# Attention and two feed-forward layers on one core: v tiles in borrowed weight slots, a rewritten order of the first group, split conversions

## The chip, the cores and the metric

The kernel runs on one core of one Trainium2 chip. The metric is the device time of one execution in microseconds (us), of which several were taken; less is better. One execution was also recorded by the hardware profiler, and all rows below come from that one.

## The reference, cut to what matters

```python
# q, k, v: (batch 4, heads 8, seq 576, head_dim 64); all float32
scores = q @ k.T / 8                  # heads 0-3: window of 32; heads 4-7: 32 keys at distance 0, 4, 8 ... 124
attn = softmax(where(mask, scores, -1e9)) @ v
x = attn.transpose(0, 2, 1, 3).reshape(2304, 512)
h = x @ w_in                          # 512 -> 2048
x = (h - tanh(h)) @ w_out             # 2048 -> 512
out = (((x @ w1) * (x @ w2)) @ w3) @ w_out2    # 512 -> 1024, 1024 -> 1024, 1024 -> 512
```

## The kernel before, in words

**Split numbers.** Each matrix operand of the feed-forward layers is held as a high part and a low part in TensorE's own 32-bit format, and a product is three matmuls (high by high, high by low, low by high). A weight arrives as raw 64-bit words and must be converted on the core: ScalarE takes an absolute value (word `a` of the list below, `cv_abs`), VectorE does two pairs of bit operations (`b` and `c`, lines 148 to 161, `cv_bits`), ScalarE writes the high part (`i`, line 166), GpSimd the low part (`o`, line 169). A weight lands in one of two staging buffers, so the third weight can be loaded only when the `c` of the first is done.

**Attention** works on 12 units (a batch and a third of the sequence), each of two types: `p`, the plain window, and `d`, the dilated one. For a unit and type, SyncE loads q and k (`q`), then v (`v`); TensorE makes the masked scores (`s`, lines 466 and 478), VectorE takes the maximum and subtracts it (`M`), ScalarE takes the exponential (`E`), VectorE sums and inverts (`N`), GpSimd multiplies (`m`), TensorE transposes (`T`, line 522), ScalarE copies (`C`), TensorE multiplies by v (`P`, line 553), ScalarE and VectorE write the high and low part of the result into `X` (`X`, `L`). The scores of the first three units are made type by type, of later units both types together.

**First layer pair.** The 16 chunks of w_in and w_out go in four groups of 3, 4, 4 and 5 chunks. In the first group the tokens go in seven tiles of 256 and one of 512, in later groups in tiles of 512 and 256. One step `i` is one chunk on one token tile: `h` (12 matmuls, line 596), `t` (tanh), `g` (subtract, line 644), `G` and `k` (high and low part), `y` (12 matmuls, line 686); after the last chunk of a group `Y` and `Z` add the four y banks into `Y` (lines 704 to 708).

**Who sets the order.** Up to the end of the first group every engine's instructions follow one list written out by hand, `ORDER`: each word is one of the letters above with a unit or step number, `S` is a run of dummy matmuls on a zero tile (`spin`, line 715), `K` prepares the masks and `w` loads a weight. Each engine runs its own instructions in that order, SyncE its loads as well: a load that must wait for a buffer holds back all loads behind it. Later a loop goes through the steps: for step i it issues `h`, `t`, `g`, `G`, then `tick()` (which converts the next weight), then the low part, then `y` of step i-1 and its four adds. The second layers follow as a loop over products, which the change does not touch.

**Buffers.** q, k and v of the first units lie in the not yet used `Y`, as far as there is room; later ones in three rotating buffers each. Before the change three of the first unit's v tiles found room there; the other three took the three rotating v buffers. `WG` holds 16 weight slots of 2 KB a partition, from the start on.

Of the kernel before, what the change touches and what calls it, by code (L numbers as in the profile page):

```python
# [45 lines left out]


ORDER = """
q0p S10 q1p K0 K1 q1d s0p S2 M0p q2p s1p E0p N0p S6 v1p M1p m0p T0p E1p q0d S1 C0p N1p s2p m1p v0p
M2p T1p S4 C1p q2d E2p s0d N2p s1d m2p v0d M0d P0p E0d M1d w0 P1p X0p N0d E1d T2p w1 X1p N1d m0d s2d  # L50
C2p L1p m1d L0p T0d v2p M2d a0 S5 C0d v1d b0 E2d T1d c0 a1 q3p S2 P2p N2d i0 P0d o0 b1 X2p w2 C1d S6
X0d q3d L2p m2d L0d P1d c1 T2d X1d v2d a2 L1d i1 b2 h0 C2d w3 o1 c2 s3 t0 q4p g0 i2 P2d M3 G0 o2 q4d
a3 h1 X2d k0 b3 E3 y0 w4 t1 c3 v3p g1 i3 s4 L2d G1 o3 N3 v3d a4 k1 h2 M4 w5 m3p m3d T3p t2 v4p g2
C3p b4 h3 G2 q5p c4 E4 P3p t3 a5 g3 k2 T3d N4 X3p v4d h4 i4 C3d o4 L3p q5d b5 t4 P3d y1 g4 m4d X3d
c5 v5p h5 G3 q6p L3d m4p i5 s5 k3 o5 t5 w6 g5 T4p M5 y2 q6d C4p P4p Y2 Z2 E5 q7p T4d y3 C4d N5 X4p
v5d P4d G4 m5p L4p G5 a6 m5d T5p v6p X4d b6 s6 C5p k5 c6 w7 T5d P5p M6 k4 q7d C5d y4 X5p i6 L5p E6
w8 o6 L4d h6 a7 N6 q8p y5 t6 b7 g6 m6d s7 c7 G6 Y5 v6d a8 Z5 k6 i7 w9 h7 b8 M7 m6p y6 q8d t7 o7 g7
E7 T6p c8 h8 q9p G7 a9 N7 k7 C6p P5d t8 w10 b9 s8 X5d m7d L5d g8 v7p m7p c9 G8 y7 q9d k8 T6d a10 P6p
C6d M8 q10p h9 X6p L6p E8 y8 b10 v7d t9 g9 P6d N8 G9 w11 Y8 k9 s9 X6d Z8 m8d L6d v8p m8p c10 T7p
q10d h10 C7p P7p t10 q11p g10 T7d G10 X7p h11 k10 M9 C7d v8d T8p t11 P7d g11 E9 w12 L7p s10 X7d N9  # L60
C8p v9p L7d m9p P8p m9d q11d T8d X8p y9 C8d L8p M10 v9d h12 G11 k11 E10 P8d t12 N10 s11 X8d v10p L8d
m10p g12 m10d h13 y10 t13 g13 y11 G12 k12 T9p Y11 Z11 h14 C9p G13 T9d k13 t14 y12 g14 C9d M11 y13
G14 k14 E11 P9p N11 P9d X9p v10d L9p m11p T10p X9d h15 v11p C10p L9d m11d T10d t15 P10p g15 C10d y14
X10p v11d G15 L10p k15 P10d Y14 Z14 T11p X10d h16 C11p L10d y15 t16 g16 G16 P11p k16 h17 X11p L11p
y16 t17 g17 G17 h18 k17 y17 t18 g18 G18 T11d k18 Y17 Z17 h19 C11d P11d t19 g19 y18 X11d G19 L11d Q0
k19 i8 h20 i9 o8 i10 y19 t20 o10 a11 g20 G20 b11 h21 k20 c11 y20 o9 t21 w13 i11 g21 o11 G21 h22 Z20
a12 Y20 k21 b12 a13 y21 t22 b13 g22 c12 G22 h23 k22 c13 i12 y22 t23 o12 i13 g23 G23 o13 h24 k23 y23
t24 g24 G24 k24 Y23 Z23
"""


# [1062 lines left out]
```

## Time and profile before

| what | value |
|---|---|
| median of 3 runs | 815.25 us (814.08 to 817.67) |
| profiled execution | 815.71 us, span of its instructions 813.9 us |
| TensorE matmuls busy | 788.7 us, 97% of the span |
| VectorE busy | 559.5 us, 69% |
| ScalarE busy | 292.4 us, 36% |
| GpSimd busy | 159.9 us, 20% |
| moved by DMA | 115.58 MB |

TensorE is the busiest engine, but its busy time includes 36 dummy matmuls and is an average over stages. The rows further down give it by stage: the start, the rest of the attention, the loop over the later groups, and the second layers.

### The profile page before, as it was taken

The numbers are of one execution on the slowest core, as the hardware profiler recorded it, in microseconds if no ns is written. First come the engines' busy times: TensorE is split into PE (matmuls) and PEld (weight loads), VectorE is DVE, ScalarE is ACT, GpSimd is POOL, SyncE is SP. The second block draws the span as 40 slices with busy tenths as digits, with TensorE's granted clock in tenths as the row PEclk, the third lists the DMA queues.
The fourth block names the chain that finished last, engine by engine and source line by source line (L and its number), as shares of the span: only waits on it lengthen the run. The fifth ranks groups of instructions, "written<-read, shape, count | busy, mean of one in ns | idle before, by whom it ended". The sixth has DMA issues, their size and how long they took to land.

```text
span 813.9 us, 14227 instructions
## 1 busy us (share of the span) xinstructions
PE 788.7 (97%) x5623; PEld 689.5 (85%) x5628; DVE 559.5 (69%) x911; ACT 292.4 (36%) x543; POOL 159.9 (20%) x155
## 2 busy tenths in 40 slices
PE   7798999999999999999999999999999999999998
PEld 4577889888878888788878788889998999899996
DVE  4889833758888888987888989964454444644441
ACT  3555645443444444443434433421123111311111
POOL 3344322600022000221022222311111111201011
PEclk9999999999999999999999999999999999999999
DMA  8999942213455254642354325187402761146402
GB/s 258 289 266 288 287 107 60 76 55 104 124 162 170 76 150 125 190 138 84 103 170 142 102 82 178 58 291 256 146 1 65 226 202 38 39 154 201 139 1 77
DMA packets 62018, 115.58 MB, mean 142 GB/s; under 512 B 6400, under 2 KB 27008, under 8 KB 61952
## 3 DMA queue, kind: packets, MB, share of 16 engines
q1 hardware_dynamic: 61664, 114.32, 46.3%
q8 instruction: 44, 0.72, 0.4%
q10 hardware_dynamic: 288, 0.36, 0.2%
q14 instruction: 22, 0.18, 0.1%
HBM read 95.26 MB, written 19.40 MB: 141 GB/s over the span
## 4 chain that ended last, share of the span: by engine, by line
PE 79%; DVE 11%; DMA 5%; issue 2%; SPq 1%; ACT 1%; ACTq 0%; DVEq 0%
PE h L596 22%; PE pr L935 22%; PE y L686 20%; PE o L998 6%; PE pr L998 6%; DVE a L158 2%; PE x L553 2%; DVE a L161 2%; DMA q<-in_qz 2%; DMA Y<-in_qz 2%; DVE a L152 1%; DVE a L148 1%; DVE th L644 1%; DVE Y L704 1%; DVE gs L658 1%
## 5 line engine op out<-in xcount | busy, mean ns | idle before, releaser
L596 PE MATMUL h<-X,WG 128*128 128x512 f32 (+1 forms) x662 | 129.0, 342 | 3.1 <-DVE th L644 3.0
L686 PE MATMUL y<-gs,LT 128*128 128x512 f32 (+1 forms) x520 | 123.0, 369 | 3.2 <-DVE Y L704 2.5
L596 PEld LDWEIGHTS h<-X,WG 128*128 128x128 f32 x662 | 105.4, 191 | 18.2 <-DVE th L644 3.7
L686 PEld LDWEIGHTS y<-gs,LT 128*128 128x128 f32 x520 | 92.0, 188 | 21.5 <-issue 4.5
L686 PE MATMUL y<-gs,WG 128*128 128x256 f32 (+1 forms) x548 | 108.4, 332 | 1.2 <-DVE Y L704 0.9
L596 PE MATMUL h<-X,LT 128*128 128x512 f32 (+1 forms) x471 | 104.7, 369 | 0.0
L596 PEld LDWEIGHTS h<-X,LT 128*128 128x128 f32 x471 | 82.8, 189 | 15.0
L686 PEld LDWEIGHTS y<-gs,WG 128*128 128x128 f32 x548 | 85.1, 189 | 12.2 <-issue 1.4
L644 DVE TENSOR_TENSOR th<-h,th 128x512 f32<-128x512 f32 (+1 forms) x83 | 51.2, 617 | 58.8 <-ACT th L638 58.6
L638 ACT ACTIVATE th<-h 128x512 f32<-128x512 f32 (+1 forms) x83 | 44.8, 540 | 124.5 <-PE h L596 123.3
L161 DVE SCALAR_TENSOR_TENSOR a<-st,a 128x512 uint32<-128x512 uint32 x68 | 80.8, 1188 | 2.3
L935 PE MATMUL pr<-X 128*128 128x384 f32 x435 | 81.9, 335 | 0.0
L935 PE MATMUL pr<-X,LT 128*128 128x384 f32 x405 | 80.3, 335 | 0.0
L935 PEld LDWEIGHTS pr<-X 128*128 128x128 f32 x435 | 76.3, 188 | 0.5
L651 ACT ACTIVATE gs<-th 128x512 fp32r<-128x512 f32 (+1 forms) x83 | 47.7, 576 | 70.2 <-DVE th L644 67.1
L935 PEld LDWEIGHTS pr<-X,LT 128*128 128x128 f32 x405 | 71.4, 188 | 1.3
L972 DVE TENSOR_TENSOR u<-pr,u 128x384 f32<-128x384 f32 x72 | 40.1, 557 | 45.6 <-PE pr L935 38.9
L990 POOL TENSOR_TENSOR Y<-w,v 128x384 f32<-128x384 f32 x24 | 24.4, 1019 | 213.1 <-DVE w L972 213.1
L948 ACT ACTIVATE cs<-u 128x384 fp32r<-128x384 f32 x24 | 12.6, 526 | 148.6 <-DVE u L972 148.6
L143 ACT ACTIVATE a<-st 128x512 f32<-128x512 f32 x68 | 45.5, 669 | 31.1 <-DMA st<-in_w_out 10.0
L169 POOL TENSOR_TENSOR LT<-a,LT 128x512 fp32r<-128x512 f32 x18 | 25.2, 1402 | 157.1 <-ACT LT L166 155.1
L158 DVE SCALAR_TENSOR_TENSOR a<-st,a 128x512 uint32<-128x512 uint32 x68 | 53.6, 789 | 2.1
(132 smaller groups left out, 1077.4 us busy)
## 6 DMA issues: line engine op xcount, KB each, us to landing
st<-in_w SPq DMA_DIRECT2D x28, 512.0 KB, 3.5
LT<-p SPq DMA_DIRECT2D x56, 256.0 KB, 4.4
X<-p SPq DMA_DIRECT2D x56, 256.0 KB, 4.9
st<-in_w_in SPq DMA_DIRECT2D x16, 512.0 KB, 4.4
st<-in_w_out SPq DMA_DIRECT2D x16, 512.0 KB, 4.2
p<-WG SPq DMA_DIRECT2D x30, 256.0 KB, 4.6
q<-in_qz SPq DMA_DIRECT2D x19, 384.0 KB, 6.6
p<-LT SPq DMA_DIRECT2D x26, 256.0 KB, 4.6
```

Of the source, the lines that this page charges most:

```text
L143: nc.scalar.activation(out=a.bitcast(F32), in_=st[:, :, 1].bitcast(F32), func=ACTF.Abs)
L158: nc.vector.scalar_tensor_tensor(out=a, in0=st[:, :, 1], scalar=0xC0000000, in1=a, op0=ALU.bitwise_and, op1=ALU.bitwise_or)
L161: nc.vector.scalar_tensor_tensor(out=a, in0=st[:, :, 0], scalar=29, in1=a, op0=ALU.logical_shift_right, op1=ALU.bitwise_or)
L169: nc.gpsimd.tensor_tensor(out=lo, in0=a.bitcast(F32), in1=hi.bitcast(F32), op=ALU.subtract)
L596: nc.tensor.matmul(out=ps, lhsT=a[sel[0]], rhs=b[sel[1]], start=(start and i == 0), stop=(i == n - 1), **kw)
L638: nc.scalar.activation(out=th[:, :tn], in_=gst[i][:, :tn], func=ACTF.Tanh)
L644: nc.vector.tensor_tensor(out=th[:, :tn], in0=ps[:, :tn], in1=th[:, :tn], op=ALU.subtract)
L651: nc.scalar.activation(out=gs[:, 0, :tn], in_=th[:, :tn], func=ACTF.Copy)
L686: nc.tensor.matmul(out=y[k], lhsT=wt[sel[0]][:, 128 * k:128 * k + 128], rhs=gs[:, sel[1], tn * m:tn * m + tn], start=(cs[m] == 0 and n == ...
L935: nc.tensor.matmul(out=ps[:, :TP], lhsT=s[e][:, 128 * k:128 * k + 128], rhs=(hi, lo)[f][1][k], start=start and n == 0, stop=n == 5, skip_g ...
L972: nc.vector.tensor_tensor(out=out, in0=ps[:, :TP], in1=x, op=op)
L998: nc.tensor.matmul(out=tiles[m], lhsT=cs[e][:, 128 * m:128 * m + 128], rhs=WW[j][f], start=begin and n == 0, stop=end and n == 2,)
```

## The change

Four edits. (1) `WG` is cut to six slots; in the bytes of the other ten a pool of six v tiles holds v of the first batch (units 0 to 2, both types), and the ten slots are opened in the same bytes by `more_slots()` when the fourth weight needs them. (2) `ORDER` is written anew, without any `S`. (3) Of the four mask casts of line 363, two go to ScalarE, with the cast of the identity. (4) In the loop `tick()` is cut in two: the first pair of bit operations stays where it was, the second pair comes after the four adds of the step before.

```diff
+NF = 6
...
-WG = big.tile([128, NW, 512], F32R, name="WG")
+WG = big.tile([128, NF, 512], F32R, name="WG")
...
-free = deque(WG[:, i, :] for i in range(NW))
+free = deque(WG[:, i, :] for i in range(NF))
...
-X0d q3d L2p m2d L0d P1d c1 T2d X1d v2d a2 L1d i1 b2 h0 C2d w3 o1 c2 s3 t0 q4p g0 i2 P2d M3 G0 o2 q4d
+P0d o0 X2p L2p o1 X0d i2 M3 P1d L0d X1d E3 a3 L1d q4p q4d h0 v2d s4 N3 C2d P2d w4 b3 t0 g0 h1 G0 c3
...
-    def tick():
+    halfway = []
+
+    def tick_begin():
         busy = bitsed and split()
         if not busy and absed and len(free) >= slots_for(absed[0][0]) + reserve[0]:
             key, st, a = absed.popleft()
-            cv_bits(st, a)
+            cv_bits(st, a, 0)
+            halfway.append((key, st, a, [free.popleft() for _ in range(slots_for(key))]))
+
+    def tick_end():
+        if halfway:
+            key, st, a, slots = halfway.pop()
+            cv_bits(st, a, 1)
             done.add(key)
-            bitsed.append((key, a, [free.popleft() for _ in range(slots_for(key))]))
+            bitsed.append((key, a, slots))
         prefetch()
         store_parked()
...
-            window_of(1, 3, 1, 1, by_dve)
-            by_dve(id16_sb, id_sb)
+            window_of(1, 3, 1, 1, by_act, (2, 3))
+            by_act(id16_sb, id_sb)
+            window_of(1, 3, 1, 1, by_dve, (0, 1))
...
+    vh = ExitStack()
+    vh_pool = vh.enter_context(tc.tile_pool(name="vh", bufs=1, side="right"))
+    vhomes = [vh_pool.tile([128, 2 * TU * 2 * D], F32, tag=f"v{m}", name=f"v{m}") for m in range(2 * PB)]
+    def v_home(n):
+        if n < PB:
+            return vhomes.pop(0)
+        return attn_pools["vv"].tile([128, 2 * TU * 2 * D], F32, tag="v", name="v")
+    def more_slots():
+        vh.close()
+        p = ctx.enter_context(tc.tile_pool(name="wh", bufs=1, side="right", reuse_waits="tile"))
+        free.extend(p.tile([128, 512], F32R, tag=f"w{m}", name=f"w{m}") for m in range(NW - NF))
...
-                if i == N0 or width(i) == 512:
-                    tick()
+                ticks = i == N0 or width(i) == 512
+                if ticks:
+                    tick_begin()
                 if i > N0:
                     st_glo(i)
             if i > N0:
                 st_y(i - 1)
                 st_evac(i - 1, 0)
                 st_evac(i - 1, 1)
+            if i < NS and ticks:
+                tick_end()
             phase()
```

What the two lists put ahead of a step, counted from their words (scores counted by unit and type):

| ahead of | list | s | T | P | h | y | c | MB up to the load that it needs last |
|---|---|---|---|---|---|---|---|---|
| h0 | before | 6 | 6 | 5 | 0 | 0 | 2 | 7.04 (v of unit 1, type d) |
| h0 | after | 8 | 6 | 5 | 0 | 0 | 3 | 8.75 (the same) |
| s4 | after | 8 | 6 | 5 | 1 | 0 | 3 | 10.52 (q of unit 4, type d) |
| s11 | before | 22 | 18 | 18 | 13 | 10 | 11 | 29.33 (q of unit 11, type d) |
| s11 | after | 22 | 20 | 18 | 14 | 12 | 9 | 26.97 (the same) |
| h14 | before | 24 | 19 | 18 | 14 | 12 | 11 | |
| h14 | after | 24 | 21 | 19 | 14 | 13 | 10 | |

The bytes follow from the shapes: q and k of a unit and type 0.59 MB (first unit of a batch) or 0.62 MB, v 0.39 MB, a weight 0.52 MB, the masks and the identity 0.36 MB. Ahead of the third weight (`w2`) the list after asks for 6.85 MB, up to and with the first for 3.93 MB.

The next rows are SyncE's queue before the change, from the v of unit 0, type d, to the q of unit 3, type d (`k` and `q` are loads from in_kT and in_qz, `v` from in_vt, `st` weights).

```order
L425 DMA v<-in_vt 64x2x128
L425 DMA v<-in_vt 64x2x256
L425 DMA v<-in_vt 64x2x128
L425 DMA v<-in_vt 64x2x256
L138 DMA st<-in_w_in 128x1024 x2
L425 DMA v<-in_vt 64x2x384 x4
L402 DMA k<-in_kT 128x2x192
L405 DMA q<-in_qz 128x2x384
L138 DMA st<-in_w_out 128x1024
L402 DMA k<-in_kT 128x2x192
L405 DMA q<-in_qz 128x2x384
```

The same stretch after the change, from the v of unit 2, type p, to that of unit 1, type d.

```order
L453 DMA v_101<-in_vt 64x2x384 x2
L430 DMA k<-in_kT 128x2x192
L433 DMA q<-in_qz 128x2x384
L138 DMA st<-in_w_out 128x1024
L430 DMA k<-in_kT 128x2x192
L433 DMA q<-in_qz 128x2x384
L453 DMA v_102<-in_vt 64x2x128
L453 DMA v_102<-in_vt 64x2x256
L453 DMA v_102<-in_vt 64x2x128
L453 DMA v_102<-in_vt 64x2x256
L453 DMA v_103<-in_vt 64x2x384 x2
```

Here v of the first batch goes to tiles of its own (`v_101` and so on); q and k of unit 3, both types, and the third weight (`st<-in_w_out`) now stand ahead of the v loads of type d.

TensorE before the change, from the last dummy matmuls ahead of the first step `h0` (the first row with `h<-X`) to `h1`; `s` rows are the scores of unit 3, `x` rows are `P`.

```order
L715 LDWEIGHTS warm
L715 MATMUL h<-warm 128x512
L553 MATMUL x<-pb,v 64x2x32 x12
L522 MATMUL t<-id_sb,Y 128x128 x3
L596 MATMUL h<-X,WG 128x256 x12
L466 LDWEIGHTS id_sb
L466 MATMUL s<-mask_sb,id_sb 128x384
L466 LDWEIGHTS id_sb
L466 MATMUL s<-mask_sb,id_sb 128x384
L478 MATMUL s<-k,q 32x64 x48
L553 MATMUL x<-pb,v 64x2x32 x12
L596 MATMUL h<-X,WG 128x256 x12
```

After the change, from the last scores of unit 3 to `h1`.

```order
L506 MATMUL s<-k,q 32x64 x48
L550 MATMUL t<-id_sb,Y 128x128 x3
L581 MATMUL x<-pb,v_102 64x2x32 x12
L581 MATMUL x<-pb,v_103 64x2x32 x12
L624 MATMUL h<-X,WG 128x256 x12
L494 LDWEIGHTS id_sb
L494 MATMUL s<-mask_sb,id_sb 128x384
L494 LDWEIGHTS id_sb
L494 MATMUL s<-mask_sb,id_sb 128x384
L506 MATMUL s<-k,q 32x64 x48
L581 MATMUL x<-pb,v_104 64x2x32 x12
L624 MATMUL h<-X,WG 128x256 x12
```

The dummy matmuls are gone, the scores of unit 3 stand ahead of `h0`, and those of unit 4 (rows L494 and L506 behind `h0`) stand between `h0` and `h1`.

VectorE in the loop before the change, one step that ends a token tile (`gs` is the low part, `Y` rows the four adds).

```order
L644 TENSOR_TENSOR th<-h,th 128x512
L148 TENSOR_SCALAR a<-a 128x512
L152 TENSOR_SCALAR a<-a 128x512
L158 SCALAR_TENSOR_TENSOR a<-st,a 128x512
L161 SCALAR_TENSOR_TENSOR a<-st,a 128x512
L658 TENSOR_TENSOR gs<-th,gs 128x512
L704 TENSOR_TENSOR Y<-y_3988,Y 128x512
L704 TENSOR_TENSOR Y<-y_3989,Y 128x512
L704 TENSOR_TENSOR Y<-y_3990,Y 128x512
L704 TENSOR_TENSOR Y<-y_3991,Y 128x512
L644 TENSOR_TENSOR th<-h,th 128x512
```

The same after the change.

```order
L672 TENSOR_TENSOR th<-h,th 128x512
L148 TENSOR_SCALAR a<-a 128x512
L152 TENSOR_SCALAR a<-a 128x512
L686 TENSOR_TENSOR gs<-th,gs 128x512
L732 TENSOR_TENSOR Y<-y_3953,Y 128x512
L732 TENSOR_TENSOR Y<-y_3954,Y 128x512
L732 TENSOR_TENSOR Y<-y_3955,Y 128x512
L732 TENSOR_TENSOR Y<-y_3956,Y 128x512
L158 SCALAR_TENSOR_TENSOR a<-st,a 128x512
L161 SCALAR_TENSOR_TENSOR a<-st,a 128x512
L672 TENSOR_TENSOR th<-h,th 128x512
```

The rows L158 and L161 moved from ahead of the low part and the adds to behind them.

## Rows read from the trace of the kernel before

**Rows 1.** Busy time by stretch; columns: engine busy (instructions), granted clock, DMA share, GB/s.

```profile
0.00:34.00 34.00, 24.67 (x467) 15.50 (x473) 21.38 (x49) 13.69 (x26) 11.30 (x25) 0.95 0.93 272
34.00:125.00 91.00, 84.16 (x1646) 75.31 (x1645) 70.90 (x120) 51.32 (x110) 36.44 (x40) 0.98 0.82 235
125.00:500.00 375.00, 370.85 (x1923) 313.96 (x1922) 304.74 (x482) 160.86 (x285) 66.82 (x51) 1.00 0.41 121
```

**Rows 2.** Timeline to 10 us: start, length, instructions, idle before.

```profile
1.32 3.78 PE L715 MATMUL h<-warm 128*128 128x512 bf16 x10 [1.32 <-POOL warm L780]
...
4.12 0.94 DVE L363 CAST mask_sb<-Y 32x128 bf16<-32x128 f32 x4 [4.12 <-DMA Y<-in_masks]
```

**Rows 3.** Timeline of TensorE, 30 to 62 us.

```profile
33.32 1.93 PE L596 MATMUL h<-X,WG 128*128 128x256 f32 x12
...
41.59 0.50 PE L466 MATMUL s<-mask_sb,id_sb 128*128 128x384 bf16 x2
...
43.50 1.77 PE L596 MATMUL h<-X,WG 128*128 128x256 f32 x12
...
48.65 0.92 PE L553 MATMUL x<-pb,v 128*64 128x64 f32 x24
49.49 0.55 PE L522 MATMUL t<-id_sb,pm 128*128 128x128 f32 x3
50.03 1.69 PE L596 MATMUL h<-X,WG 128*128 128x256 f32 x12
...
58.78 1.67 PE L686 MATMUL y<-gs,WG 128*128 128x256 f32 x12
60.38 0.92 PE L553 MATMUL x<-pb,v 128*64 128x64 f32 x24
```

**Rows 4.** Timeline of TensorE, 108 to 119 us.

```profile
109.85 1.33 PE L478 MATMUL s<-k,q 128*32 128x64 f32 x48 [1.85 <-DMA q<-in_qz]
111.11 2.76 PE L596 MATMUL h<-X,WG 128*128 128x256 f32 x12
...
116.82 1.68 PE L596 MATMUL h<-X,WG 128*128 128x256 f32 x12
```

**Rows 5.** Waits of TensorE, 34 to 125 us: total, times, longest.

```profile
PE h L596 <- DVE th L644: 3.0, 2, 2.5
PE s L478 <- DMA q<-in_qz: 2.5, 2, 1.8
```

**Rows 6.** Chain that ended last, to 30 us: start, length, two loads.

```profile
1.25 4.43 DMA Y<-in_qz
...
7.93 8.31 DMA Y<-in_qz
```

**Rows 7.** Busy time by stretch, columns as in rows 1.

```profile
24.00:28.00 4.00, 1.30 (x17) 0.86 (x19) 3.65 (x8) 2.96 (x6) 0.73 (x1) 1.00 1.07 233
28.00:32.00 4.00, 3.78 (x49) 2.55 (x45) 3.45 (x6) 1.83 (x4) 1.50 (x2) 0.57 1.07 378
```

**Rows 8.** Waits of TensorE, 125 to 500 us.

```profile
PE y L686 <- DVE Y L704: 3.4, 7, 0.6
PE y L686 <- DVE gs L658: 0.6, 1, 0.6
```

**Rows 9.** Timeline of VectorE and TensorE around one wait in the loop.

```profile
230.44 0.42 DVE L148 TENSOR_SCALAR a<-a 128x512 f32<-128x512 f32 x1
...
231.36 0.69 DVE L158 SCALAR_TENSOR_TENSOR a<-st,a 128x512 uint32<-128x512 uint32 x1
...
232.08 1.67 DVE L161 SCALAR_TENSOR_TENSOR a<-st,a 128x512 uint32<-128x512 uint32 x1
...
233.68 0.68 DVE L658 TENSOR_TENSOR gs<-th,gs 128x512 fp32r<-128x512 f32 x1
...
234.28 1.88 DVE L704 TENSOR_TENSOR Y<-y,Y 128x512 f32<-128x512 f32 x3
...
235.10 1.17 PE L686 MATMUL y<-gs,WG 128*128 128x512 f32 x4 [0.50 <-DVE Y L704]
```

More of the change, by code (lines that the diff above doesn't have):

```diff
@@ L48 @@
 ORDER = """
-q0p S10 q1p K0 K1 q1d s0p S2 M0p q2p s1p E0p N0p S6 v1p M1p m0p T0p E1p q0d S1 C0p N1p s2p m1p v0p
-M2p T1p S4 C1p q2d E2p s0d N2p s1d m2p v0d M0d P0p E0d M1d w0 P1p X0p N0d E1d T2p w1 X1p N1d m0d s2d
-C2p L1p m1d L0p T0d v2p M2d a0 S5 C0d v1d b0 E2d T1d c0 a1 q3p S2 P2p N2d i0 P0d o0 b1 X2p w2 C1d S6
-X0d q3d L2p m2d L0d P1d c1 T2d X1d v2d a2 L1d i1 b2 h0 C2d w3 o1 c2 s3 t0 q4p g0 i2 P2d M3 G0 o2 q4d
-a3 h1 X2d k0 b3 E3 y0 w4 t1 c3 v3p g1 i3 s4 L2d G1 o3 N3 v3d a4 k1 h2 M4 w5 m3p m3d T3p t2 v4p g2
@@ L54 @@
[L54 to L68, printed above, removed]
+K0 K1 q0p q1p s0p q2p q0d M0p q1d s1p E0p s2p s0d M1p N0p m0p w0 T0p E1p C0p N1p M2p q2d M0d E2p m1p
@@ new lines @@
+N2p T1p v0p s1d v1p m2p s2d w1 a0 E0d C1p T2p b0 P0p C2p N0d c0 M1d X0p M2d E1d v2p a1 m0d L0p b1
+T0d q3p E2d P1p C0d w2 a2 q3d P2p N1d c1 m1d T1d s3 N2d C1d i0 m2d i1 T2d b2 c2 v0d v1d X1p L1p w3
+P0d o0 X2p L2p o1 X0d i2 M3 P1d L0d X1d E3 a3 L1d q4p q4d h0 v2d s4 N3 C2d P2d w4 b3 t0 g0 h1 G0 c3
+i3 X2d M4 t1 a4 m3p T3p k0 o2 L2d q5p E4 q5d g1 o3 y0 w5 h2 v3p q6p G1 s5 C3p v3d b4 c4 t2 k1 m3d
+T3d g2 q6d i4 o4 a5 N4 C3d h3 m4p M5 t3 E5 b5 P3p c5 v4p T4p v4d C4p y1 N5 X3p L3p g3 P3d G2 X3d m4d
@@ new lines @@
+T4d i5 k2 C4d L3d s6 M6 q7p q7d o5 P4p v5p X4p L4p h4 t4 m5p y2 Y2 G3 E6 P4d X4d w6 g4 h5 T5p Z2 C5p
+m5d s7 N6 G4 L4d v5d P5p k3 y3 t5 g5 a6 X5p G5 T5d C5d w7 k4 a7 b6 k5 v6p m6p L5p y4 h6 M7 q8p t6
+T6p c6 g6 q8d y5 q9p C6p i6 h7 G6 v6d E7 b7 t7 c7 g7 P5d N7 k6 w8 G7 Y5 m6d s8 q9d X5d P6p X6p Z5
+T6d k7 h8 v7p m7p y6 L5d C6d P6d t8 M8 a8 E8 g8 G8 q10p m7d h9 N8 m8p X6d v7d T7p C7p s9 T7d o6 k8
+t9 g9 y7 C7d h10 M9 t10 L6p g10 T8p G9 v8p E9 i7 N9 b8 P7p L6d X7p w9 y8 h11 k9 m8d L7p Y8 q10d s10
@@ new lines @@
+q11p G10 t11 C8p m9p P7d g11 q11d Z8 X7d P8p X8p L7d L8p T8d k10 y9 G11 M10 h12 c8 y10 E10 k11 C8d
+t12 v8d m9d v9p a9 v9d y11 w10 T9p C9p g12 h13 G12 P8d b9 Y11 k12 Z11 t13 N10 m10p g13 T9d m10d G13
+s11 M11 P9p X8d L8d C9d X9p k13 c9 E11 y12 w11 T10p h14 y13 C10p T10d t14 g14 a10 b10 G14 P9d k14
+N11 m11p L9p C10d v10p h15 t15 v10d y14 g15 G15 Y14 h16 v11p T11p t16 k15 Z14 g16 y15 X9d o7 L9d G16
+k16 m11d P10p X10p h17 C11p c10 t17 v11d P10d g17 G17 y16 L10p X10d T11d C11d h18 a11 t18 P11p X11p
@@ L69 @@
+L10d L11p P11d k17 X11d w12 g18 y17 L11d Y17 b11 Q0 i8 G18 i9 c11 h19 Z17 k18 t19 o8 g19 h20 G19 h21
+w13 t20 y18 k19 i10 y19 h22 g20 t21 g21 G20 G21 k20 i11 k21 y20 a12 h23 b12 o9 a13 b13 t22 g22 G22
+o10 o11 Z20 k22 Y20 h24 c12 t23 c13 g23 i12 y21 G23 y22 o12 k23 i13 y23 t24 g24 G24 o13 k24 Z23 Y23
 """
@@ L295, in tick @@
             absed.append((key, st, cv_abs(st)))
+    def tick():
+        tick_begin()
+        tick_end()
     def phase():
@@ L350, in prep_masks, with window_of @@
         m = attn_pools["m"]
-        def window_of(a, b, to, step, copy):
-            for j in range(4):
+        def window_of(a, b, to, step, copy, js=range(4)):
+            for j in js:
                 r = slice(HQ * j, HQ * j + HQ)
@@ L417, in load_v @@
             for ty in parts:
-                v = home(n, 2 * TU * 2 * D, "vv", "v").rearrange("p (h t c) -> p h t c", h=2, t=TU)
+                v = v_home(n).rearrange("p (h t c) -> p h t c", h=2, t=TU)
                 for e in range(2):
@@ L732, in high @@
         def high(m):
+            if 2 * m == NF:
+                more_slots()
             hl[m] = free.popleft(), free.popleft()
@@ L794, in attn_moe_kernel @@
                     st_ghi(i)
-                if i == N0 or width(i) == 512:
-                    tick()
+                ticks = i == N0 or width(i) == 512
+                if ticks:
+                    tick_begin()
                 if i > N0:
@@ L802, in attn_moe_kernel @@
                 st_evac(i - 1, 1)
+            if i < NS and ticks:
+                tick_end()
             phase()
```

## The prediction

> **What bounds the kernel now.** I read the stages first [rows 1]: each row gives the busy time of the five engines in one stretch. TensorE is busy for 24.67 of the first 34 us, 84.16 of the next 91 and 370.85 of the 375 of the loop; behind 500 us no written order changes. So the loop can give back 375 - 370.85 = 4.15 us at most, and the rest must come from the first 125 us, in which the DMA engines are nearly full (share 0.93 and 0.82 of the stretches).
>
> Busy time flatters the start, since the dummy matmuls count in it: the first ten take 3.78 us [rows 2]. I therefore use another measure, the **lost time** at a step: its start in the trace less the useful TensorE work that the written order puts ahead of it. Work that is put off is still to be done, so only lost time moves the end. The prices are spacings of starts [rows 3]: two scores 43.50 - 41.59 = 1.91, so 0.96 each; P 49.49 - 48.65 = 0.84; T 50.03 - 49.49 = 0.54, taken as 0.5; y 60.38 - 58.78 = 1.60, and h, the same twelve matmuls of 128x256, the same. With the counts of the table of the change:
>
> - h0 before: 6 x 0.96 + 6 x 0.5 + 5 x 0.84 = 13.0 us of work; it starts at 33.32 [rows 3]; lost 20.3.
> - s11 before, second type: 23 x 0.96 + 18 x 0.5 + 18 x 0.84 + 23 x 1.6 = 83.0; it starts at 109.85 [rows 4]; lost 26.9.
> - h14 before: 24 x 0.96 + 19 x 0.5 + 18 x 0.84 + 26 x 1.6 = 89.3; it starts at 116.82 [rows 4]; lost 27.5.
>
> So 20 us are lost ahead of the first step, and 7 more up to h14. Of those 7, the waits name 3.0 for VectorE's subtraction of line 644 (one of 2.5) and 2.5 for q, of which 1.85 ahead of s11 [rows 4, 5]. Behind that wait h takes 2.76 us where it takes 1.68 a little later [rows 4]: TensorE ran at its lower level. From 125 us on nothing waits but the y matmuls for the adds of line 704, seven times, 3.4 us, and once 0.6 for a low part [rows 8].
>
> **The start (edits 1 and 2).** The new order loads more ahead of h0 and works off more: 8.75 MB instead of 7.04 up to the last load that h0 needs, and two more scores. What must land next is q of unit 4, 10.52 MB, since s4 now stands between h0 and h1. Rate: 272 GB/s over the first 34 us [rows 1], with a share of 0.93, so 272 / 0.93 = 292 without gaps. v tiles of their own take away what held SyncE back, waits for a v buffer, but not the wait of the third weight for its staging buffer. Landing lags the bytes: the q issued at 7.93 took 8.31 us and landed at 16.24 [rows 6], with 3.80 MB asked for up to it, which at 272 GB/s counted from 2 us on (my choice) are there at 16.0; at 292 GB/s, at 15.0; so it lags by 0.2 to 1.2. For s4: 2 + 10.52 / 0.292 + 1.2 = 39.2; without gaps the rate of the best stretch, 378 for q and weights, and 233 for a stretch with v [rows 7], would give 2 + 8.55 / 0.378 + 1.97 / 0.233 + 0.2 = 33.3; with gaps, at 272 and the greater lag, 41.9. I take 39, near the rate of the whole start, since the mix of loads is the same. Work ahead of s4: 8 x 0.96 + 3.0 + 4.2 + 1.6 = 16.5. **Lost at s4: 22.5** (17 to 25.4), more than the 20.3 at h0 before. For h0 itself this means about 34 to 36 us, as it is now; the new order does not start the first step earlier, it starts it with more in stock.
>
> **The dummy matmuls (edit 2).** 36 of them go. Their time, at 3.78 / 10 apiece up to 13.6 us, is no gain as such: they stand where TensorE waits for loads, and lost time counts them already. What they bought is the clock. The granted clock was 0.57 in 28 to 32 us, behind a stretch of 4 us in which TensorE was busy for 1.30 [rows 7], and 0.98 over the next 91 us [rows 1]. Without them the first dense run, from about h0 on, will start at the lower of the two levels (1.2 and 2.4 GHz). The price of one such restart is on record: from s11 (109.85) to h14 (116.82) are 6.97 us for 0.96 + 1.6 + 3.2 + 0.5 = 6.3 us of work [rows 4], so 0.7. I put 1.0; below, nothing (the run begins behind s4's wait anyway, where loads set the pace), above, 3 restarts, 2.1. The Trainium skill, page "TensorE: Matmul & The Clock Gate", section "Why this matters for your kernels", says that idle gaps between bursts of matmuls put TensorE back to its lower clock and that one should warm it up ahead; the trace agrees on the first (0.57 behind the sparse stretch). It speaks against this edit; what it would make of the time is the third rival.
>
> **From h0 to h14 (edit 2).** Here the list takes strain away. Ahead of s11 stand 26.97 MB instead of 29.33: at 292 GB/s its q lands 8 us earlier, and TensorE has two y, one h and two T more to do ahead of it (3.2 + 1.6 + 1.0 = 5.8 us). The 1.85 us wait and the 0.7 behind it go; nothing near it needs a load so late. On VectorE nine conversions (`c`) instead of eleven stand ahead of s11, each 232.08 + 1.67 - 230.44 = 3.3 us from first to last operation [rows 9]: some 6.6 us of the 70.90 that VectorE is busy in 34 to 125 [rows 1], which moves behind 110 us, where it has room. So the 3.0 us for line 644 go too, in most part. I leave 2 us of the 7.2 for waits that I can't place (0 to 4: none, or as many as the rows of now less the two above). **Lost at h14: 22.5 + 1 + 2 = 25.5, against 27.5: 2.0 us gained**, between 17 + 0 + 0 (10 gained) and 25.4 + 2.1 + 4 (4 lost). I don't believe the lower end: it needs every load at its best rate, while VectorE, with three conversions ahead of h0 instead of two, then holds h0 back. A gain of 6 is as far as I go.
>
> **The mask casts (edit 3)** shorten VectorE's part ahead of the first scores, but those wait for their q, issued at 1.25 and landed 4.43 us later, at 5.68, while the four casts are done at 4.12 + 0.94 = 5.06 [rows 2, 6]. I count nothing; with the cover gone it would be half of the 0.94.
>
> **The loop (edit 4).** Look at one of the seven waits [rows 9]: VectorE does the whole conversion from 230.44 to 233.75, then the low part, and starts the four adds at 234.28; y waits 0.50 until 235.10 for the first. The y matmuls before, sorted by bank, had filled the first bank long before 231.7. With the second pair (0.69 and 1.67) put off, the low part can begin about 2.3 us earlier and the first add with it: that is more than 0.50, so the wait goes. What is late next: the second pair comes behind the four adds (1.88 us for three, so 2.5) and the low part's 0.68, and the subtraction of the next step queues behind it; its y comes a whole step later, so there is room. Of 3.4 + 0.6 us [rows 8] I take **3.5 gained**; lower bound 1.0, if only the waits beside plain adds go and those beside w1 and w2's combinations stay; upper 4.15 [rows 1]. The second pair also moves away from GpSimd's subtraction; that only shortens VectorE.
>
> **Sum.** 815.71 is the time of the profiled execution (span 813.9 and 1.8 around it), 0.46 above the median of the runs. 815.71 - 2.0 - 3.5 = 810.2 in its terms, 809.75 against the median; I say **810**.
>
> **Rivals.**
> - *Both gains in full.* Loads run at 320 GB/s because SyncE no longer waits, s4 starts at 36, and the restart costs nothing: 4 to 5 us more, 805.5. For it: the share of 0.93 has room. Against: the third weight still waits for `c0`.
> - *The start eats its gain.* The third weight waits for `c0`, and the v of type d, which h0 needs, wait behind it. The 6.85 MB ahead of it are there at 2 + 6.85 / 0.292 = 25.5; each us by which `c0` ends later leaves the DMA engines idle, and s4 comes a us later. Two or more, s4 at 41 or behind it, and the start gains nothing: 811 to 815. For it: VectorE has twelve other operations on scores around `c0`, each waiting for a load. Against: the first weight, which `c0` needs, has landed by 2 + 3.93 / 0.292 + 1.2 = 16.7, 9 us before that point.
> - *Slower, the clock.* Without dummy matmuls TensorE stays at its lower level behind h0. h costs 2.76 instead of 1.68 [rows 4], so 39% of the time at the low level is lost. To be 4 us slower in all, the loop's 3.5 and the start's 2.0 must be overcome: 9.5 us, so 24 us of dense work at the low level beyond the one counted, that is up to 65 us. Time 820. For it: loads still set the pace behind h0, with gaps. Against: one run of 7 us got the clock back now [rows 4].
> - *The change does not do what it says.* The loop's waits have another cause (the adds themselves, 1.88 us for three [rows 9]), and the start only trades dummy matmuls for idle time: 814 to 817.
>
> **How the numbers follow.** A measurement of this kernel tells about 0.5% from no change, 4.1 us, so faster is below 811.2 and slower above 819.3. The forecast (806 to 813, centre 810) has 0.50, three quarters of it below 811.2; both gains in full 0.13; the start eats its gain 0.22, a fifth of it below 811.2; no effect 0.08; slower 0.07. Faster: 0.375 + 0.13 + 0.045 = 0.55; slower 0.07; same 0.38. The range 804.5 to 815.5 leaves out the slow rival, half of no effect and the far end of the best case, under 2 in 10.
>
> **What would show it.** The start: s4 at about 39 with a wait for q, and no wait for q near s11. The clock: below 1 in the windows around h0, and at 1 by 45 us. The list: no wait of over 1 us for line 644. The loop: of the waits of y for the adds at most 1 us left. Wrong it would be if h14 starts later than now with more than 92.7 + 27.5 = 120.2 us (work ahead of it after: 24 x 0.96 + 21 x 0.5 + 19 x 0.84 + 27 x 1.6 = 92.7), or if the loop's waits stay.

## The result and the profile after

| kernel | median of the runs | ratio to before, 95% interval |
|---|---|---|
| before | 815.81 us (814.08 to 817.67) | |
| after | 805.13 us (804.05 to 806.19) | 0.9874 (0.9849 to 0.9899) |

The profiled execution took 806.19 us, its span is 804.4. By the medians the change saves 10.7 us; the forecast's terms add up to 5.5, and the result lies at the quick edge of its range.

Busy time by stretch of the kernel after, columns as in rows 1, and then the clock's stretches around h0:

```profile
0.00:34.00 34.00, 21.42 (x494) 16.15 (x496) 23.65 (x49) 14.27 (x28) 13.94 (x26) 0.87 0.98 281
34.00:125.00 91.00, 87.23 (x1658) 80.81 (x1654) 68.49 (x121) 53.72 (x118) 36.33 (x41) 0.97 0.82 232
125.00:500.00 375.00, 375.00 (x1902) 316.55 (x1903) 302.75 (x494) 162.15 (x284) 65.96 (x52) 1.00 0.41 124
...
24.00:28.00 4.00, 2.35 (x28) 2.13 (x29) 3.86 (x9) 1.34 (x4) 1.11 (x1) 0.63 1.07 351
28.00:32.00 4.00, 3.13 (x88) 2.30 (x89) 3.71 (x7) 3.65 (x7) 2.67 (x3) 0.50 0.92 203
32.00:36.00 4.00, 4.00 (x75) 3.40 (x65) 3.77 (x6) 1.04 (x3) 1.64 (x1) 0.59 0.94 283
36.00:40.00 4.00, 2.96 (x62) 2.18 (x61) 3.37 (x8) 2.88 (x6) 0.83 (x1) 1.00 1.04 266
40.00:44.00 4.00, 2.44 (x73) 2.22 (x73) 3.76 (x5) 1.05 (x2) 3.31 (x3) 0.76 1.06 338
44.00:48.00 4.00, 4.00 (x28) 4.00 (x29) 1.64 (x4) 2.15 (x5) 0.32 (x1) 0.81 0.98 294
48.00:52.00 4.00, 4.00 (x118) 3.55 (x117) 3.90 (x6) 3.00 (x8) 3.54 (x3) 1.00 0.68 192
```

Against [rows 1], TensorE is less busy in the start (no dummy matmuls), 3 us busier up to 125 us, and never idle in the loop's 375 us. Its granted clock is low from 24 to 36 us and again, in part, from 40 to 48.

The waits of TensorE from 34 to 125 us in the kernel after:

```profile
PE s L506 <- DMA q<-in_qz: 1.6, 1, 1.6
PE s L506 <- issue: 1.2, 1, 1.2
PE x L581 <- DMA v<-in_vt: 0.8, 1, 0.8
...
```

Against [rows 5], nothing waits for VectorE's subtraction any more, and q is waited for once. Where, the timeline of TensorE says:

```profile
35.75 0.50 PE L624 MATMUL h<-X,WG 128*128 128x256 f32 x2
...
38.25 0.88 PE L506 MATMUL s<-k,q 128*32 128x64 f32 x48
40.74 0.88 PE L506 MATMUL s<-k,q 128*32 128x64 f32 x48 [1.61 <-DMA q<-in_qz]
42.44 1.55 PE L581 MATMUL x<-pb,v 128*64 128x64 f32 x24 [0.83 <-DMA v<-in_vt]
43.92 2.38 PE L624 MATMUL h<-X,WG 128*128 128x256 f32 x12
...
46.39 1.67 PE L714 MATMUL y<-gs,WG 128*128 128x256 f32 x12
47.89 1.56 PE L624 MATMUL h<-X,w 128*128 128x256 f32 x12
49.30 0.50 PE L494 MATMUL s<-mask_sb,id_sb 128*128 128x384 bf16 x2
...
51.21 0.55 PE L550 MATMUL t<-id_sb,pm 128*128 128x128 f32 x3
51.51 0.72 PE L624 MATMUL h<-X,WG 128*128 128x256 f32 x4
...
113.68 1.65 PE L624 MATMUL h<-X,w 128*128 128x256 f32 x12
```

The wait for q stands in s4, between its two types. h0 starts at 35.75, later than before's 33.32 [rows 3], and h14 at 113.68, where before had 116.82 [rows 4] with less work ahead of it.

To see where the end moved, I cut each profiled execution at three instructions: the end of the first group's last evacuation, the last add of the loop, and the first matmul of the products. These are the instructions, of before and then of after:

```profile
166.61 1.28 DVE L708 COPY Y<-y 128x512 f32<-128x512 f32 x2
...
490.13 1.50 DVE L704 TENSOR_TENSOR Y<-y,Y 128x256 f32<-128x256 f32 x4 [1.39 <-PE y L686]
...
535.80 1.23 PE L935 MATMUL pr<-X,LT 128*128 128x384 f32 x6
```

```profile
159.77 1.39 DVE L736 COPY Y<-y 128x512 f32<-128x512 f32 x2 [0.74 <-PE y L714]
...
479.07 1.50 DVE L732 TENSOR_TENSOR Y<-y,Y 128x256 f32<-128x256 f32 x4 [0.70 <-PE y L714]
...
524.88 1.22 PE L968 MATMUL pr<-X,LT 128*128 128x384 f32 x6
```

So the first group ends at 167.9 and 161.2 (6.7 gained), the loop takes 323.7 and 319.4 (4.3 gained), the stage between loop and products 44.2 and 44.3, and the products to the end of the span 278.1 and 279.5: **1.4 lost**, in a stage that the change does not touch. The same cuts for every run follow; the last three columns repeat to 0.05 us between kernels whose code there and tile addresses are equal. The whole times of one kernel's runs lie several us apart, so that spread is put down to the first group, though each kernel has only one profiled execution.

| run | median us | ratio (95%) | first group ends | loop | between | products |
|---|---|---|---|---|---|---|
| before | 815.81 | | 167.9 | 323.74 | 44.17 | 278.10 |
| after | 805.13 | 0.9874 (0.9849 to 0.9899) | 161.2 | 319.41 | 44.31 | 279.52 |
| a_again | 805.49 | 0.9879 (0.9859 to 0.9898) | 161.3 | 319.42 | 44.31 | 279.51 |
| e1_loop_only | 808.48 | 0.9907 (0.9882 to 0.9932) | 166.1 | 316.90 | 44.17 | 278.08 |
| e2_no_halves | 810.34 | 0.9920 (0.9899 to 0.9942) | 159.4 | 326.14 | 44.35 | 279.49 |
| e4_before_no_dummies | 817.64 | 1.0008 (0.9984 to 1.0032) | 167.7 | 323.71 | 44.17 | 278.09 |
| e5_v_homes_only | 819.86 | 1.0051 (1.0031 to 1.0071) | 167.9 | 326.21 | 44.27 | 279.21 |
| e6_late_weights | 812.39 | 0.9966 (0.9944 to 0.9988) | 161.6 | 323.70 | 44.18 | 278.09 |
| e7_order_no_v_homes | 800.55 | 0.9821 (0.9805 to 0.9837) | 160.5 | 317.47 | 44.18 | 278.02 |
| e8_h1_first | 806.88 | 0.9904 (0.9887 to 0.9921) | 162.6 | 319.41 | 44.35 | 279.47 |
| e9_dummies_back | 806.19 | 0.9888 (0.9856 to 0.9919) | 160.2 | 319.41 | 44.32 | 279.54 |
| e3_aligned | 803.10 | 0.9860 (0.9840 to 0.9880) | 158.4 | 318.36 | 44.32 | 279.23 |
| e11_aligned_128 | 804.91 | 0.9870 (0.9841 to 0.9898) | 159.8 | 320.42 | 44.28 | 279.38 |
| e12_slots_32_off | 811.39 | 0.9952 (0.9934 to 0.9970) | 163.2 | 323.20 | 44.35 | 280.37 |

The first group by the medians: median less 1.8 us around the span, less the three fixed stages. It is 168.0 before (815.81 - 1.8 - 646.0) and 160.1 after (805.13 - 1.8 - 643.2): 7.9 gained.

### The profile page after: what moved, and what is told of

The parts are those of the page before. It is cut to its first block, busy times and chain, and to the rows that moved or that the text cites. A ratio compares the mean times of both kernels' runs of the same rounds, so it can differ in the third digit from the quotient of the medians.

```text
span 804.4 us, 14176 instructions
## 1 busy us (share of the span) xinstructions
PE 783.8 (97%) x5592; PEld 689.7 (86%) x5592; DVE 546.7 (68%) x908; ACT 292.6 (36%) x546; POOL 159.4 (20%) x155
## 4 chain that ended last, share of the span: by engine, by line
PE 90%; DMA 5%; DVE 4%; ACT 1%; SPq 1%; issue 0%; ACTq 0%
PE h L624 26%; PE y L714 25%; PE pr L968 22%; PE o L1031 6%; PE pr L1031 6%; PE x L581 2%; DMA v<-in_vt 2%; PE s L506 1%; DMA q<-in_qz 1%; DVE a L158 1%; PE t L550 1%; DMA Y<-in_qz 1%; DVE a L161 1%; DVE Y L861 1%; DVE X L875 0%; DVE a L148 0%
## 5 line engine op out<-in xcount | busy, mean ns | idle before, releaser
L624 PEld LDWEIGHTS h<-X,LT 128*128 128x128 f32 x471 | 82.8, 188 | 15.1
L624 PE MATMUL h<-X,w 128*128 128x512 f32 (+1 forms) x381 | 79.6, 354 | 0.0
L158 DVE SCALAR_TENSOR_TENSOR a<-st,a 128x512 uint32<-128x512 uint32 x68 | 73.6, 1082 | 0.3
L624 PEld LDWEIGHTS h<-X,w 128*128 128x128 f32 x381 | 62.8, 188 | 11.4
L714 PE MATMUL y<-gs,w 128*128 128x256 f32 (+1 forms) x352 | 70.9, 331 | 0.0
L714 PEld LDWEIGHTS y<-gs,w 128*128 128x128 f32 x352 | 54.6, 188 | 7.1
L161 DVE SCALAR_TENSOR_TENSOR a<-st,a 128x512 uint32<-128x512 uint32 x68 | 54.8, 806 | 2.3
```

Of the source, the lines that this page charges most:

```text
L158: nc.vector.scalar_tensor_tensor(out=a, in0=st[:, :, 1], scalar=0xC0000000, in1=a, op0=ALU.bitwise_and, op1=ALU.bitwise_or)
L161: nc.vector.scalar_tensor_tensor(out=a, in0=st[:, :, 0], scalar=29, in1=a, op0=ALU.logical_shift_right, op1=ALU.bitwise_or)
L624: nc.tensor.matmul(out=ps, lhsT=a[sel[0]], rhs=b[sel[1]], start=(start and i == 0), stop=(i == n - 1), **kw)
L714: nc.tensor.matmul(out=y[k], lhsT=wt[sel[0]][:, 128 * k:128 * k + 128], rhs=gs[:, sel[1], tn * m:tn * m + tn], start=(cs[m] == 0 and n == ...
```

## The experiments

**e1_loop_only: the halves in the kernel before.**

```diff
-                    tick()
+                    tick_begin()
...
+            if i < NS and ticks:
+                tick_end()
```

> The kernel before with edit 4 alone. Theory A (the adds of the step before were late, lost time is given back one for one): the waits of y for the adds (3.4 us) and for the low part (0.6) go from the loop, 811.8 us. Rival (the halves only help behind the new order, which leaves the loop another stock of weights): at most one of the seven waits goes, 815 us.

The loop takes 316.90 instead of 323.74: the halves alone bring 6.8 us, twice the 3.5 forecast and more than the bound of 4.15. In the loop's stretch TensorE has no idle time left. Why the bound did not hold is in the starts of its steps before the change, around the wait of [rows 9], and then comes e1's row of the loop's stretch:

```profile
226.28 2.88 PE L596 MATMUL h<-X,WG 128*128 128x512 f32 x12
229.00 2.88 PE L686 MATMUL y<-gs,LT 128*128 128x512 f32 x12
231.72 2.88 PE L596 MATMUL h<-X,LT 128*128 128x512 f32 x12
```

```profile
125.00:500.00 375.00, 375.00 (x1930) 319.68 (x1929) 302.26 (x493) 163.02 (x288) 64.38 (x52) 1.00 0.40 122
```

Without a wait, h to y takes 229.00 - 226.28 = 2.72. With it, 235.10 - 231.72 = 3.38: the end moves by 0.66, where the row says 0.50. The same count, from start to start, over all 130 steps of the loop gives the whole gain. Before, four h of 512 tokens take 3.38 to 3.44 us and six y 2.80 to 2.85, where all others take 2.72 to 2.75; three h of 256 tokens take 1.98 to 2.10 and three y 1.73 to 2.33, where the others take 1.43 to 1.50. In e1 none takes more than 2.75 and 1.44. The sum of the differences is 6.8 us. Matmuls overlap in the records, so the idle column shows less than a wait moves the next start.

**e2_no_halves: the changed kernel without edit 4.**

```diff
-                    tick_begin()
+                    tick()
...
-            if i < NS and ticks:
-                tick_end()
```

> The changed kernel with edit 4 undone, conversions whole again. Theory A: the waits of y for the adds come back, 3 to 4 us over the changed kernel, 808.5 to 809. Rival: the loop's gain was none of edit 4's, 805 to 806.

The waits of TensorE in 125 to 500 us are back:

```profile
PE y L701 <- DVE Y L719: 3.2, 7, 0.6
PE y L701 <- DVE gs L673: 0.7, 1, 0.7
```

The loop is 6.7 us longer than in the kernel after (326.14), yet also 2.4 longer than before, with the same code in the loop. On the whole it takes 810.34 us, 5 more than the change and over theory A's 809. So edits 1 to 3 hold something that makes the loop slower.

**a_again: the changed kernel once more,** beside others on one chip.

> The changed kernel once more, unaltered, so that the next three have it on their chip: 804 to 806.

It repeats to 0.4 us, and the fixed stages to 0.01.

**e4_before_no_dummies: the list before without its 36 dummy matmuls.**

```diff
-ORDER = """ ... S10 ... S3 ... S6 ... S4 ...
+ORDER without any S
```

> The kernel before with its 36 dummy matmuls left out of the list, nothing else. Theory A (they stand where TensorE waits for loads, so their 10.6 us are no gain; the clock costs about 1, and some 2 us of them that delayed P ahead of the first step come back): 814 to 816.5. Rival B (the dummy matmuls were the loss): 808 or less. Rival C (the clock rule: without them TensorE stays slow behind the first step): 818 to 822.

Ratio 1.0008, with an interval from 1.3 us quicker to 2.6 us slower: no difference that these runs can tell. The clock is lower in the start (0.90 against 0.95) and not later:

```profile
0.00:34.00 34.00, 21.27 (x438) 16.70 (x438) 21.61 (x50) 13.86 (x27) 11.29 (x25) 0.90 0.94 269
34.00:125.00 91.00, 82.85 (x1645) 74.04 (x1644) 70.27 (x120) 51.22 (x109) 36.89 (x40) 1.00 0.81 237
```

**e9_dummies_back: 23 of them in the new list.**

```diff
-K0 K1 q0p ... s0p q2p ... q3d P2p ... T1d s3
+K0 K1 S10 q0p ... s0p S3 q2p ... q3d S6 P2p ... T1d S4 s3
```

> The changed kernel with the 23 dummy matmuls of the kernel before put back into the waits of the start (ten behind the masks of the first step, three behind s0p, six before P2p, four before s3). Theory A, they keep the clock granted but stand in waits, and the clock costs little there: 804.5 to 806.5, no different from the changed kernel, with a granted clock of 0.95 and over to 34 us. Rival B, the clock that fell to 0.5 to 0.8 around 24 to 48 us costs what the prediction gave it at the upper bound: 2 us come back, 802.5 to 804. Rival C, they stand ahead of work that has its data and push it: 806.5 to 808.

806.19, no different from the change (theory A's time). Its clock expectation failed: the dummies did not hold it at 0.95 to 34 us, it was 0.85. They moved the low stretch ahead: from 32 us on the clock is at 1, where the change without them has 0.59, 0.76 and 0.81.

```profile
0.00:34.00 34.00, 25.10 (x503) 15.59 (x505) 21.22 (x48) 14.27 (x28) 11.98 (x26) 0.85 0.95 276
...
32.00:36.00 4.00, 3.72 (x149) 3.28 (x140) 2.82 (x5) 2.74 (x7) 2.52 (x2) 1.00 1.04 315
...
40.00:44.00 4.00, 2.65 (x79) 2.48 (x80) 3.86 (x6) 1.54 (x3) 3.06 (x3) 1.00 1.05 340
```

**e6_late_weights: in the list before, the last weights of the first group later.**

```diff
-w10, w11, w12, a10, b10 and c10 where the list before has them
+q11d w10 w11 ... t13 a10 ... Z11 b10 ... t14 c10 ... G14 w12
```

> The kernel before with three of its prefetched weights (the 11th to 13th) asked for behind the last q instead of ahead of it, and the 11th's conversion behind h13. Theory A (between h0 and h14 it was the place of weights and conversions that cost): the wait for q ahead of s11 and the restart behind it go, 2.5 to 4 us, 812 to 813.5. Rival (what counted was v of its own tiles and SyncE not held back): 815 to 816.

Ratio 0.9966. Its profiled execution was one of the quick ones (first group 161.6); by the median the first group is 812.39 - 1.8 - 646.0 = 164.6, so this move alone gains some 3 us in the list before (1.0 to 4.6 by the interval of the ratio). Its waits of TensorE in 34 to 125 us, the two rows on which the forecast rested:

```profile
PE h L596 <- DVE th L644: 2.0, 2, 1.6
...
PE s L478 <- DMA q<-in_qz: 0.5, 1, 0.5
```

q falls from 2.5 [rows 5] to 0.5, line 644 from 3.0 to 2.0.

**e8_h1_first: the new list, with s4 and P2d behind h1.**

```diff
-h0 v2d s4 N3 C2d P2d w4 b3 t0 g0 h1 G0
+h0 v2d N3 C2d w4 b3 t0 g0 h1 s4 P2d G0
```

> The changed kernel with the scores of unit 4 and P of unit 2, type d, put behind h1 instead of ahead of it. Theory (h1 has what it needs and would fill the 1.6 us wait of s4 for its q and the 0.8 of P for its v): 1 to 2 us less than the changed kernel, 803 to 804. Rival (the loads set the pace for longer, the wait comes back at s5): 805.

It failed: 806.88, 1.4 over a_again on the same chip. The wait for q ahead of s4 is gone, and h1, now right behind h0, waits for VectorE's subtraction in its place:

```profile
39.43 2.82 PE L625 MATMUL h<-X,WG 128*128 128x256 f32 x12 [2.23 <-DVE th L673]
```

So s4 between h0 and h1 is in its place: it covers a wait of 2.23 us for that subtraction, the kind of wait that [rows 5] showed.

**e5_v_homes_only: edits 1 and 3 with the list before and without the halves,** the ten slots at a multiple of 128 bytes.

```diff
+NF = 6
...
+    def v_home(n):
+        if n < PB:
+            return vhomes.pop(0)
...
-            window_of(1, 3, 1, 1, by_dve)
+            window_of(1, 3, 1, 1, by_act, (2, 3))
```

> The kernel before with the homes for v (the ten slots at a multiple of 128 bytes) and with the mask casts that may go to ScalarE, but with its own written order and without the halves. Theory A, the written order alone made the first group faster, and homes and casts free nothing that it waited for: 814 to 817, the loop 323.7, the products 278.1. Rival, the early v loads that no longer wait for a buffer bring the first group 2 to 4 us by themselves: 811.5 to 813.5 with the same loop and products.

Both theories were wrong on the whole, 819.86, because the loop and the products grew (326.21 and 279.21). The first group is as long as before, 167.9: with this list, homes and casts bring it nothing.

**e7_order_no_v_homes: the changed kernel without edit 1.** `WG` has its sixteen slots in one piece again, and all six v tiles of the first batch take the three rotating buffers: its trace has no load of v into `Y`. (In the kernel before, the loads of v into `Y` make two tiles, not three; the other four took the rotating buffers.)

```diff
-        if n < PB:
-            return vhomes.pop(0)
-        return attn_pools["vv"].tile([128, 2 * TU * 2 * D], F32, tag="v", name="v")
+        return home(n, 2 * TU * 2 * D, "vv", "v")
...
-WG = big.tile([128, NF, 512], F32R, name="WG")
+WG = big.tile([128, NW, 512], F32R, name="WG")
```

> The changed kernel without edit 1: WG keeps 16 slots in one piece, and v of the first batch takes turns in the three rotating buffers; the new list, the casts and the halves stay. Theory A (the list is what counts: by the changed kernel's trace a v buffer is free before its next load comes to its turn, P of unit 0 at 19.4 us and that load at 23.4): no loss from v, and the slots stay at multiples of 64 bytes, 801 to 802.5. Rival B (v tiles of their own keep SyncE going): 806 or more.

800.55, **the quickest of all**, 4.6 to 4.9 us below the change. The first group is as short as with the homes, and loop and products are back near e1's. Of the loop, 0.6 us over e1's 316.90 is left; it comes with edits 2 and 3, and its cause stays open.

**e3_aligned, e11_aligned_128, e12_slots_32_off: where the slots lie.** The traces hold no addresses; these are the ones that the built programs give their tiles. In the kernel before `X`, `WG`, `Y`, `LT` and the tiles of `gs` start at a multiple of 512 bytes. After the change the ten new slots start 480 bytes behind one. e3 and e11 leave bytes empty beside the ten slots, which puts them 448 and 384 bytes behind one. e12 shifts the sixteen slots of e7 in one piece by 32 bytes, and with them all tiles that lie behind, `LT` and `gs` among them, by 128; `X` stays.

```diff
+    ctx.enter_context(tc.tile_pool(name="pad", bufs=1, side="right")).tile([128, 8], F32, name="pad")
...
+    ... tile([128, 24], F32, name="pad")
...
+    pads = [big.tile([128, 8], F32, name="pad0")]
     WG = big.tile([128, NW, 512], F32R, name="WG")
+    pads.append(big.tile([128, 24], F32, name="pad1"))
```

> The changed kernel with a pad of 32 bytes a partition at the top of SBUF, so that the ten slots of the new pool start at multiples of 64 bytes, as WG, LT and X do, and not 32 bytes off. Theory (matmuls that read such a slot take longer: 394 to 397 ns instead of 389 to 390 at 512 columns, and the three stages behind the first group were 2.5, 0.15 and 1.4 us longer than with WG in one piece): 4 us less than the changed kernel, 801. Rival (the slots' place has nothing to do with it, the longer stages come from another order of the slots): 804 to 806.

> The changed kernel with 96 bytes left empty beside the ten new slots, so that they start at a multiple of 128 bytes; nothing else. With 32 bytes left empty (a multiple of 64) the stage of the rotated loop took 318.36 us and the products 279.23, about half of the way back from 319.4 and 279.5 to the 317.5 and 278.0 of the kernel without homes for v. Theory A, the time of a matmul goes by how its tile lies to 128 bytes: the loop takes 317.0 to 317.6, the products 278.0 to 278.2, matmuls out of the new slots 389 to 390 ns, whole 799 to 801.5. Rival, what is left of the loss lies in the two allocations as such and not in the address: 318.3 and 279.2 again, whole 801.5 to 804.

> The kernel of the new order without homes for v (800.55 us, loop 317.47, products 278.02), its sixteen weight slots shifted by 32 bytes in one piece, all other tiles at a multiple of 128 bytes as before. Theory A, the address alone costs: in the changed kernel ten of sixteen slots lie so and cost 2.0 us in the loop, 0.15 in the stage behind it and 1.5 in the products, so sixteen cost some 3.1, 0.25 and 2.3: loop 320 to 321.5, products 280 to 281, whole 805 to 807.5, matmuls out of the slots 394 to 397 ns. Rival, the split of the slots costs and the address is nothing: loop 317.4, products 278.0, whole 799.5 to 801.5.

Costliest groups of TensorE with shapes apart (line, names, count | busy, mean ns of one), of e7, after, e3, e11 and e12:

```profile
L613 PE MATMUL h<-X,LT 128*128 128x512 f32 x383 | 93.4, 389 | 0.0
L613 PE MATMUL h<-X,WG 128*128 128x512 f32 x342 | 83.3, 389 | 0.0
L955 PE MATMUL pr<-X,WG 128*128 128x384 f32 x144 | 30.7, 334 | 0.0
```

```profile
L624 PE MATMUL h<-X,LT 128*128 128x512 f32 x383 | 93.5, 390 | 0.0
L624 PE MATMUL h<-X,w 128*128 128x512 f32 x245 | 61.3, 394 | 0.0
L968 PE MATMUL pr<-X,w 128*128 128x384 f32 x144 | 31.3, 339 | 0.0
```

```profile
L625 PE MATMUL h<-X,w 128*128 128x512 f32 x245 | 60.5, 392 | 0.0
```

```profile
L625 PE MATMUL h<-X,w 128*128 128x512 f32 x245 | 61.4, 395 | 0.0
```

```profile
L615 PE MATMUL h<-X,LT 128*128 128x512 f32 x383 | 95.5, 394 | 0.0
L615 PE MATMUL h<-X,WG 128*128 128x512 f32 x342 | 85.2, 395 | 0.0
```

e12 shows that the address by itself costs: a plain shift of the tiles brings 5.7 us in the loop and 2.4 in the products, 811.39 against 800.55, with no wait of TensorE from 125 to 500 us. The starts say the same as the lengths, which overlap: two matmuls of 512 columns that both read `WG` start 227 ns apart in e7 and 233 in e12, and 233 apart in the change where both read new slots. Theory A's 807.5 is passed by 3.9 us. Some of it goes with LT, which I had taken for unharmed: shifted by 128 bytes, its 383 matmuls of h, whose other operand `X` did not move, go from 389 to 394 ns as well. But by the medians 2.6 us lie in the first group, where nothing uses LT; they stay open. A rule of 64 or 128 bytes falls: e11, at a multiple of 128, is no better than the change (395 ns, loop 320.42, of which 0.6 is a wait for a weight), and e3, at a multiple of 64 alone, gave back half of the loss in the loop and a fifth of that in the products.

In the h and y of the loop, in each run by itself, the groups at a multiple of 512 bytes are the quick ones and those at the other starts the slower, with one exception: in e3 the matmuls of h out of `WG`, at a multiple of 512, take 392 like those out of the new slots. In the last layer the start does not sort them so well: `pr<-LT,WG` goes from 389 in e7 to 393 in the change with both tiles at a multiple of 512, and `o<-LT,cs` takes 393 in e7 and 391 in e12, where both tiles are shifted. So that the start of the stationary tile alone decides is not shown. The slots are read as `lhsT` in slices of 128 columns of 4 bytes, 512 bytes a partition, so a start at a multiple of 512 keeps each slice within one piece of 512; but the weight loads take 188 ns in the change from old slots and new, so their rows do not show how it comes about, and the new slots at a multiple of 512 were not tried.

## Why the prediction was right in sign and half in size

**The loop, "3.5 gained".** The mechanism is as described (e1, e2). Here it is in the kernel after, VectorE's rows around the same step:

```profile
224.75 0.42 DVE L148 TENSOR_SCALAR a<-a 128x512 f32<-128x512 f32 x1
225.20 0.43 DVE L152 TENSOR_SCALAR a<-a 128x512 uint32<-128x512 uint32 x1
225.54 0.68 DVE L686 TENSOR_TENSOR gs<-th,gs 128x512 fp32r<-128x512 f32 x1
226.14 2.47 DVE L732 TENSOR_TENSOR Y<-y,Y 128x512 f32<-128x512 f32 x4
228.54 0.68 DVE L158 SCALAR_TENSOR_TENSOR a<-st,a 128x512 uint32<-128x512 uint32 x1
229.25 0.69 DVE L161 SCALAR_TENSOR_TENSOR a<-st,a 128x512 uint32<-128x512 uint32 x1
```

The low part begins 0.8 us behind the start of the conversion, the adds follow at once, and the second pair comes behind them. The term was mis-sized: it is 6.8 in the kernel before (e1) and 6.7 in the one after (e2), because a wait costs more in starts than its idle row says. The upper bound of 4.15 rested on that column and was no bound.

**The weight slots, a term that the sum did not have.** Edit 1 was costed for its loads and not for where the new tiles lie. That cost is 1.9 in the loop (319.41 against 317.47 in e7), 0.1 and 1.5 in the stages behind it: 3.6 of the fixed stages. By the medians e7 is 4.6 to 4.9 quicker than the change; the rest of that lies in the first group and may be spread. The two misses have opposite signs, so the loop's net of 4.3 looks nearer to 3.5 than it was.

**The first group, "2.0 gained".** It is 6.7 in the profiled executions, 7.9 by the medians. The start came out as forecast: h0 at 35.75 (forecast 34 to 36), s4 at 38.25 and 40.74 (39). The third weight did not run SyncE dry: the rate of the first stretch rose to 281 GB/s and its DMA share to 0.98, so neither "the start eats its gain" nor the 320 GB/s of "both gains in full" happened; that rival's 805.5 was hit by other causes. The step that failed is the one before: "20 us are lost ahead of the first step, and 7 more up to h14". By the forecast's own prices the kernel after has lost 40.74 - 17.4 = 23.3 at the second half of s4 (forecast 22.5) and 113.68 - 92.7 = 21.0 at h14; but lost time can't shrink, so the prices were too high. They were spacings that themselves held waits. In the dense stretch of the timeline after, T takes 51.51 - 51.21 = 0.30 instead of 0.5, h 49.30 - 47.89 = 1.41 and y 47.89 - 46.39 = 1.50 instead of 1.6, two scores 51.21 - 49.30 = 1.91 as before. (The clock was 0.81 in part of that stretch; in e9, at 1, the same y and h take 1.52 and 1.40.) With 0.95 for s, 0.3 for T, 0.85 for P and 1.5 for h and y, before has lost 33.32 - 11.75 = 21.6 at h0 and 116.82 - 82.8 = 34.0 at h14, 12.4 in between and not 7. After has lost 40.74 - 16.1 = 24.6 at the second half of s4 and 113.68 - 85.75 = 27.9 at h14, 3.3 in between: the 1 + 2 us that the forecast left over were right. The gain, 34.0 - 27.9 = 6.1, was there to be had because more was being lost than I saw.

**What in the list brought it.** The list alone, since e5 (homes and casts without it) brings the first group nothing and e7 (list and casts without homes) all of it: 800.55 - 1.8 - 639.7 = 159.1 by the median, 8.9 under before. Against the kernel before on e7's own chip (815.31) it is 8.4. So the v tiles of their own, which the forecast credited with taking away SyncE's waits, were not needed: e7's v takes the rotating buffers. The later weights are worth some 3 us in the list before (e6), as the forecast argued from 29.33 and 26.97 MB. That they bring as much in the new list, and that the other 5 or so come from the remaining moves together, is an inference from the difference; one of these moves is s4's place, which covers h1's wait (e8), and I did not take them apart further.

**The dummy matmuls and the clock.** The restart, put at 1.0, could not be told from nothing in the medians, which tell some 2 us: without them before is the same (e4), with them after is the same (e9). The rows show a price of that size: h1 of the change, at 43.92, takes 2.38 us, where the h at 47.89 takes 1.56. The clock was to be at 1 by 45 us; it was 0.81 from 44 to 48 and 1 from 48, so that sign came 3 us late. The Trainium skill, page "TensorE: Matmul & The Clock Gate", section "Why this matters for your kernels", has idle gaps between bursts of matmuls bring the lower clock. The rows of after agree: TensorE is busy for 2.35 of the 4 us from 24 to 28, at a clock of 0.63, and 0.50 and 0.59 follow up to 36; the second dip, from 40 to 48, stands behind waits of 1.61 and 0.83 us. Its advice to warm TensorE up first, given there for benchmarks, brought nothing here that the medians show, in either list.

**The mask casts, 0.** Nothing speaks against it: e5 has them and its first group ends where before's does. No run has the casts alone.
